# Two key tiles' scores, then two tiles' value products: an attention loop of a two-layer transformer on one NeuronCore

## The chip, the core and the metric

The kernel runs on one core of one Trainium2 chip. The metric is the time of one execution on the device in microseconds (us). Lower is better. The engines are named PE (TensorE, matrix products; PEld is its weight load), ACT (ScalarE), DVE (VectorE), POOL (GpSimd) and SP (SyncE, which here issues DMA transfers).

## The reference

The work is two layers, each an attention block and a gated feed-forward block, with the same weights in both layers. The sequence has 2048 rows of width 448. There are 16 query heads of width 28, and one key and one value head that all of them share.

```python
def _A_ref(x, wq, wk, wv, wo):               # x: 1 x 2048 x 448, H = 16, Dh = 28
    q = (x @ wq).reshape(B, S, H, Dh).transpose(0, 2, 1, 3)
    k = x @ wk                                # 2048 x 28, shared by the heads
    v = x @ wv
    scores = einsum("bhqd,bkd->bhqk", q, k) * (Dh ** -0.5)
    p = softmax(scores, axis=-1)
    o = einsum("bhqk,bkd->bhqd", p, v)
    return o.transpose(0, 2, 1, 3).reshape(B, S, H * Dh) @ wo

def _B_ref(x, w_gate, w_up, w_down):          # inner width 1792
    return (silu(x @ w_gate) * (x @ w_up)) @ w_down

x = x + _A_ref(layernorm(x), wq, wk, wv, wo)
x = x + _B_ref(layernorm(x), w_gate, w_up, w_down)
x = x + _A_ref(layernorm(x), wq, wk, wv, wo)
x = x + _B_ref(layernorm(x), w_gate, w_up, w_down)
```

All values are float32. Products that need more than one reduced-precision pass split an operand in a high and a low part and add up three products.

## The kernel before

**Engines and order.** The order on each engine is the order in which the program issues its instructions; nothing is rescheduled. Engines wait for each other through semaphores that follow from the use of tiles and banks. PSUM has eight banks of 128 x 512 float32. In the attention stage two groups of three banks, `threes[0]` and `threes[1]`, and two single banks, `banks[6]` and `banks[7]`, are in use.

**Attention, `scores`.** A group `i` is one block of 512 query rows and four of the 16 heads, so there are 16 groups in `GR` for each layer. A step `n = 16 i + kt` handles key tile `kt` (128 keys) of group `i`. In it:

- `step(n)`, line 564: 12 score products in three passes of four. The four heads lie in four row strips of the array (32 x 128 each) and run beside each other. Three heads write the banks of `threes[n % 2]`, the fourth writes bank 7. Then ACT takes the exponential of bank 7 into `pt1` (line 570), and of the three banks into `pt` (line 571).
- `between_steps(n)`: only at `kt == 10`, and only for groups after which four groups of one block of queries are complete (three times in each layer): the output projection (`outproj`, line 548) of 48 products into the score banks which are free, with four additions to the residual `xres` on DVE (line 552). In two of these blocks PE also transposes parts of a normalised tile (`flip`).
- `pv(n - 2)`, line 601: four products of exponentials and values, one for each head, in four column strips of the array (128 x 32 each), added up in bank 6 over the 16 key tiles of the group. The values carry a column of ones, whose sums are the softmax's denominators.
- After a group's last tile, `post(i)` copies bank 6 to SBUF (line 614, DVE) and sends the denominators through four small DMA transfers to a tile `rs` (line 617). Two steps later `rest` compares and inverts them on DVE (lines 623 to 625), spreads them with two transfers through DRAM (`rd` and `o`, lines 627 and 628), and POOL multiplies and splits the result (lines 635, 133 and 134).

**Beside the steps.** At `kt == 4` SP loads the raw queries of group `i + 2` (`stack`, `qraw`, line 377), at `kt == 7` POOL splits them (`parts`), and at `kt == 9` a transfer adds rows of maxima (`rows`, line 388). In groups 11, 12 and 13, `weights` loads and splits weights of the feed-forward block at `kt == 8`. In groups 5, 13 and 14 parts of a layer norm are issued, one in each step from `kt == 6`: four times statistics on DVE (lines 213 and 214), then `scale` on POOL (`rstd`, lines 218 and 219). In groups 5 and 13 the four `apply` on DVE (line 226) follow, from `kt == 11`; the first of them waits for `rstd`.

The program has a second copy of the whole (`full`), which is skipped at run time unless a check on the denominators asks for it; it does not run in the executions shown here.

The functions that the change touches:

Of the kernel before, what the change touches and what calls it, by code (L numbers as in the profile page):

```python
# [8 lines left out]
F32 = mybir.dt.float32  # L9
F32R = mybir.dt.float32r  # L10
AF = mybir.ActivationFunctionType
ALU = mybir.AluOpType
# [3 lines left out]
P = 128  # L16
# [6 lines left out]
NT = S // P  # L23
NC = S // 512
# [29 lines left out]
def forward(  # L54
# [14 lines left out]
    nc = tc.nc  # L69
    fine, least, whole = fine or (None, None, None)  # L70
    KC = NC
# [14 lines left out]
    phase, banks, threes, live, turn = ExitStack(), [], [], set(), {}  # L86
# [33 lines left out]
    def halves(name):  # L120

        return pers.tile([P, 2, 512], F32R, tag="halves", name=name, bufs=2)
# [9 lines left out]
    def split(hi, lo, raw):  # L132
        nc.gpsimd.tensor_scalar(hi, raw, 1.0, 0.0, ALU.mult, ALU.add)
        nc.gpsimd.tensor_tensor(lo, raw, hi, ALU.subtract)
# [6 lines left out]
    vsb = pers.tile([P, NT, 32], F32, name="vsb")  # L141
# [151 lines left out]
    def between(*pos):  # L293

        for i, po in enumerate(pos):
            nc.scalar.copy(seen[:, i : i + 1], po[:, 0:1])  # L296

    GR = [(c, g) for c in range(NC) for g in range(NG)]

    class Attention:  # L300
# [208 lines left out]
        def finish(self):  # L509

            wide.append(ALL)
            if self.layer:
                nc.scalar.activation(warm, halfn[:, 0:1], AF.Exp)
                if not full:
                    self.fetch((3, 2))
                    self.fetch((0, 1))
            while self.seen < len(self.order):
                self.project()
            if not full:
                self.maxima(NC - 1, (6,))  # L520
            for n in sorted(self.when):
                for f in self.when[n]:
                    f()
            self.advance(len(self.steps), NM + KC * LEAD)
            wide.append(LOW)

        def scores(self, ff):
            next(switch)
            with tc.tile_pool(name=f"at{self.layer}", bufs=1) as wp:
                woh = wp.tile([P, NG, D], F32R, name="woh")  # L530
                wol = wp.tile([P, NG, D], F32R, name="wol")
                on, accs, pts = {}, {}, {}
                todo, due = [], {}

                def load_wo(z):
# [20 lines left out]
                def step(n):  # L556

                    i, kt = divmod(n, NT)
                    three, one = threes[n % 2], banks[7]
                    q, k, ks = qts[i % 3], keys[kt // 4], slice(P * (kt % 4), P * (kt % 4) + P)  # L560
                    for z, (kp, part) in enumerate(((0, 0), (1, 0), (0, 1))):
                        for j in range(4):
                            js = slice(32 * j, 32 * j + 32)
                            nc.tensor.matmul(  # L564
                                three[:, j, :] if j < 3 else one, k[js, kp, ks], q[js, part, :],
                                start=(z == 0), stop=(z == 2), tile_position=(32 * j, 0),
                            )
                    pt = wp.tile([P, 3, 512], F32, name="pt", bufs=3)
                    pt1 = wp.tile([P, 512], F32, name="pt1", bufs=2 if full else 3)
                    nc.scalar.activation(pt1, one, AF.Exp, scale=SCALE)  # L570
                    nc.scalar.activation(pt, three, AF.Exp, scale=SCALE)  # L571
                    pts[n] = [*(pt[:, j, :] for j in range(3)), pt1]

                def between_steps(n):

                    i, kt = divmod(n, NT)
                    free, one = threes[(n + 1) % 2], banks[7]
                    if full:
                        self.lent = free[:, 0, :]
                        self.advance(KC)  # L580
                        if kt == 11 and i + 1 < len(GR):
                            self.places[i + 1](free[:, 1, :])
                    if not todo or kt != 10:
                        return
                    c = todo.pop()
                    ks = list({8: (0, 1), 12: (2, 3)}.get(i, ()))
                    adds = []
                    for t in (1, 2, 3):
                        if ks:
                            flip(got, X0, [ks.pop(0)], one)  # L590
                        adds.append(outproj(c, t, free[:, t - 1, :]))
                    for f in adds:
                        f()
                    outproj(c, 0, one)()

                def pv(n):
                    i, kt = divmod(n, NT)
                    if kt == 0:
                        accs[i] = banks[6]
                    for j in range(4):  # L600
                        nc.tensor.matmul(  # L601
                            accs[i][32 * j : 32 * j + 32, :], vsb[:, kt, :], pts[n][j],
                            start=(kt == 0), stop=(kt == NT - 1), skip_group_check=True,
                        )
                    del pts[n]
                    if kt == NT - 1:
                        due[n + 4] = post(i)

                def post(i):

                    c, g = GR[i]
                    out2 = halves("o2").bitcast(F32)
                    oraw, rb = out2[:, 0, :], out2[:, 1, :]
                    nc.vector.tensor_copy(oraw, accs.pop(i))
                    rs = wp.tile([P, 16], F32, name="rs", bufs=2)
                    for j in range(4):
                        nc.sync.dma_start(rs[32 * j : 32 * j + 32, :], oraw[32 * j + DH : 32 * j + DH + 1, :])

                    def rest():
                        if fine is not None:  # L620
                            under = wp.tile([P, 16], F32, name="under", bufs=2)
                            for bound, op in ((LIMIT, ALU.is_lt), (1.0 / LIMIT, ALU.is_gt)):
                                nc.vector.tensor_scalar(under, rs, bound, None, op)
                                nc.vector.tensor_tensor(fine, fine, under, ALU.mult)
                        nc.vector.reciprocal(rs, rs)
                        rd = dram.tile([4, 512], F32, name="rd", bufs=2)
                        nc.sync.dma_start(rd.rearrange("j (p n) -> (j p) n", n=16), rs)
                        nc.sync.dma_start(rb, rd[:, None, :].to_broadcast([4, 32, 512]))
                        if g == 0:
                            on[c] = (  # L630
                                wp.tile([P, NG, 512], F32R, name="onh"),
                                wp.tile([P, NG, 512], F32R, name="onl"),
                            )
                        oh, ol = on[c]
                        nc.gpsimd.tensor_tensor(rb, oraw, rb, ALU.mult)  # L635
                        split(oh[:, g, :], ol[:, g, :], rb)
                        if g == NG - 1 and c < NC - 1:
                            todo.append(c)

                    return rest  # L640
# [6 lines left out]
                last = NT * len(GR)  # L647
                for n in range(last):
                    i, kt = divmod(n, NT)
                    if kt == 4 and 2 < i + 2 < len(GR):  # L650
                        self.stack(i + 2)
                    if kt == 7 and 2 < i + 2 < len(GR):
                        self.parts(i + 2)
                    if kt == 9 and 2 < i + 2 < len(GR) and not full:
                        self.rows(i + 2)
                    if i in (2, 3) and kt == 8:
                        load_wo(i - 2)
                    if n == NT and ff.nxt:
                        ff.nxt.below(nc.sync)
                    if kt == 8 and 10 < i <= 11 + FG:  # L660
                        ff.W[i - 11] = weights(i - 11)
                    step(n)
                    if not full:
                        between_steps(n)
                    if n > 1:
                        pv(n - 2)
                    if full:
                        between_steps(n)
                    if n in due:
                        due.pop(n)()  # L670
                    if i in (5, 13, 14) and kt > 5:
                        for f in {5: fs, 13: fs1, 14: ff.second[0][:5]}[i][kt - 6 : kt - 5]:
                            f()
                for n in (last - 2, last - 1):
                    pv(n)
                self.lent = None
                next(switch)
                ff.X[0] = X0
# [236 lines left out]
    for c in range(1, NC):  # L915
        fs, got = norm_steps(c)
        n = 4 * c - 4
# [38 lines left out]
```

## Time and profile before

| what | value |
|---|---|
| median of 3 runs | 2043.97 us (2043.89 to 2044.6) |
| the profiled execution | 2044.63 us |
| its span, first to last instruction | 2042.9 us |
| mean granted clock of TensorE | 0.995 |
| layer 0, first to last exponential | 68.6 to 591.0 us of the span |
| layer 1, first to last exponential | 1078.3 to 1601.0 us of the span |

In a row of the timeline stand the start in us from the start of the span, the duration in us, the engine, the line of the kernel, the operation, its output and input by the names of tiles with their shapes, and the number of instructions that the row takes together. In brackets stands how long the engine had been idle, and what released it. In a row of the costliest groups stand the count, then the busy time in us, the mean duration in ns, and idle time in us. In a row of the stretches stand the stretch in us, its length, the busy time of PE, PEld, DVE, ACT and POOL with the number of instructions, the granted clock of TensorE, and the DMA's share and rate.

### The profile page before, as it was taken

The page shows a single profiled execution, that of the slowest core. Times are in us where ns is not written, and L with a number is a line of the kernel's source. Part 1 is how long each engine was busy: PE and PEld are TensorE (multiplying, and loading weights), DVE is VectorE, ACT ScalarE, POOL GpSimd, SP SyncE. Part 2 cuts the span into 40 slices and gives each one's busy share as a digit, 9 for nine tenths or more (in the row PEclk, how much of TensorE's full clock was granted, in tenths as well). Part 3 has the DMA queues.
Part 4 walks back from the last instruction along what each step waited for, and adds up shares of the span by engine and source line. Part 5 has one row for each costly group of instructions (what it writes and reads, how often), then busy time and mean ns, then how long its engine had stood idle before and what let it go on. Part 6 is the DMA issues. An engine that isn't in the chain of part 4 may idle for free.

```text
span 2042.9 us, 43566 instructions
## 1 busy us (share of the span) xinstructions
PE 2013.0 (99%) x18577; PEld 1263.8 (62%) x18577; DVE 460.8 (23%) x892; ACT 1311.6 (64%) x2152; POOL 534.3 (26%) x599
## 2 busy tenths in 40 slices
PE   8999999999999999999999999999999999999997
PEld 6433434334358999999883334343343689988887
DVE  7200101002115232322451001010011242222322
ACT  4799897997964333333348998979979443333332
POOL 4222111021312333333351221101132123233320
PEclk9999999999999999999999999999999999999999
DMA  5101000011100111100030110000110000111102
GB/s 162 50 22 28 21 13 22 14 35 26 32 12 19 31 31 31 31 24 18 21 105 23 29 30 12 22 12 22 33 45 10 27 16 16 31 31 31 31 1 75
DMA packets 76516, 63.47 MB, mean 31 GB/s; under 512 B 22904, under 2 KB 63224, under 8 KB 76312
## 3 DMA queue, kind: packets, MB, share of 16 engines
q1 hardware_dynamic: 76040, 60.56, 10.4%
q8 instruction: 147, 2.41, 0.5%
q14 instruction: 57, 0.47, 0.1%
q10 hardware_dynamic: 272, 0.03, 0.0%
HBM read 47.72 MB, written 12.32 MB: 29 GB/s over the span
## 4 chain that ended last, share of the span: by engine, by line
PE 48%; ACT 46%; issue 1%; DVE 1%; DMA 0%; POOL 0%; ACTq 0%; POOLq 0%; DVEq 0%
PE bank L289 39%; ACT pt L571 31%; ACT pt L570 15%; PE bank L269 3%; PE three L548 2%; PE bank L548 2%; PE bank L243 1%; PE bank L601 1%; PE three L564 1%; DVE xres L735 0%; DVE sg L821 0%; DVE h L825 0%; DVE xn L226 0%; ACT h L822 0%; ACT sg L820 0%
## 5 line engine op out<-in xcount | busy, mean ns | idle before, releaser
L571 ACT ACTIVATE pt<-three 128x1536 f32<-128x1536 f32 x512 | 741.3, 1448 | 0.0
L601 PE MATMUL bank<-pt,vsb 128*32 128x512 f32 x4096 | 547.5, 607 | 0.5 <-ACT pt L571 0.5
L564 PEld LDWEIGHTS three<-qstack,keys 32*128 32x128 f32 x4608 | 253.5, 184 | 448.5 <-ACT pt L570 392.4
L564 PE MATMUL three<-qstack,keys 32*128 32x512 f32 x4608 | 500.4, 427 | 0.5 <-ACT pt L571 0.4
L564 PE MATMUL bank<-qstack,keys 32*128 32x512 f32 x1536 | 494.4, 427 | 4.0 <-ACT pt L570 4.0
L289 PE MATMUL bank<-xh,wgh 64*128 64x512 f32 x1728 | 456.4, 390 | 0.4
L289 PE MATMUL bank<-xh,wgl 64*128 64x512 f32 x1404 | 374.0, 390 | 0.0
L570 ACT ACTIVATE pt<-bank 128x512 f32<-128x512 f32 x512 | 305.9, 597 | 77.9 <-PE bank L564 71.0
L289 PE MATMUL bank<-xl,wgh 64*128 64x512 f32 x1296 | 341.6, 390 | 0.0
L289 PE MATMUL bank<-wdh,h 64*128 64x448 f32 x1792 | 335.3, 364 | 1.4 <-ACT h L822 0.8
L289 PEld LDWEIGHTS bank<-xh,wgh 64*128 64x128 f32 x1728 | 270.1, 184 | 20.1 <-DVE xl L250 1.5
L289 PEld LDWEIGHTS bank<-wdh,h 64*128 64x128 f32 x1792 | 248.0, 184 | 17.9 <-issue 2.7
L739 POOL TENSOR_TENSOR xres<-stage,xres 128x448 f32<-128x448 f32 x108 | 127.4, 1199 | 499.6 <-ACT stage L738 499.6
L635 POOL TENSOR_TENSOR o<-o 128x512 f32<-128x512 f32 x32 | 41.1, 1283 | 826.7 <-DMA o<-rd 756.8
L564 PEld LDWEIGHTS bank<-qstack,keys 32*128 32x128 f32 x1536 | 244.6, 184 | 5.4 <-ACT pt L570 5.1
L296 ACT COPY seen<-bank 128x1 f32<-128x1 f32 x664 | 82.2, 163 | 247.1 <-PE bank L289 244.1
L289 PEld LDWEIGHTS bank<-xh,wgl 64*128 64x128 f32 x1404 | 222.0, 184 | 14.5
L289 PE MATMUL bank<-wdl,h 64*128 64x448 f32 x896 | 222.8, 367 | 0.0
L820 ACT ACTIVATE sg<-bank 128x512 f32<-128x512 f32 x112 | 67.3, 601 | 220.5 <-PE bank L289 215.4
L289 PEld LDWEIGHTS bank<-xl,wgh 64*128 64x128 f32 x1296 | 201.7, 184 | 11.1
L601 PEld LDWEIGHTS bank<-pt,vsb 128*32 128x32 f32 x4096 | 80.9, 108 | 191.0 <-issue 176.3
L821 DVE TENSOR_TENSOR sg<-bank,sg 128x512 f32<-128x512 f32 x112 | 77.5, 692 | 501.1 <-ACT sg L820 492.1
(113 smaller groups left out, 1722.7 us busy)
## 6 DMA issues: line engine op xcount, KB each, us to landing
o<-rd SPq DMA_DIRECT2D x32, 256.0 KB
qd<-stage SPq DMA_DIRECT2D x32, 224.0 KB
qraw<-qd SPq DMA_DIRECT2D x128, 56.0 KB
wdr<-in_B_w_down_dram SPq DMA_DIRECT2D x28, 224.0 KB
wr<-in_B_w_gate_dram SPq DMA_DIRECT2D x28, 192.0 KB
wr<-in_B_w_up_dram SPq DMA_DIRECT2D x28, 192.0 KB
out_dram<-xres SPq DMA_DIRECT2D x16, 224.0 KB
xres<-in_A_x_dram SPq DMA_DIRECT2D x3, 896.0 KB
```

The lines of the kernel that those rows point to most:

```text
L269: nc.tensor.matmul(po, a, b, start=(i == 0), stop=(i == len(seq) - 1))
L289: nc.tensor.matmul(po, a, b, start=start, stop=stop, skip_group_check=True)
L296: nc.scalar.copy(seen[:, i : i + 1], po[:, 0:1])
L548: nc.tensor.matmul(po[:, 0:D], a[:, g, ts_], b[:, g, :], start=(g + z == 0), stop=(g == NG - 1 and z == 2))
L564: nc.tensor.matmul(three[:, j, :] if j < 3 else one, k[js, kp, ks], q[js, part, :], start=(z == 0), stop=(z == 2), tile_position=(32 * j, 0),)
L570: nc.scalar.activation(pt1, one, AF.Exp, scale=SCALE)
L571: nc.scalar.activation(pt, three, AF.Exp, scale=SCALE)
L601: nc.tensor.matmul(accs[i][32 * j : 32 * j + 32, :], vsb[:, kt, :], pts[n][j], start=(kt == 0), stop=(kt == NT - 1), skip_group_check=True,)
L635: nc.gpsimd.tensor_tensor(rb, oraw, rb, ALU.mult)
L739: nc.gpsimd.tensor_tensor(r, s, r, ALU.add)
L820: nc.scalar.activation(sg, pg[0], AF.Silu)
L821: nc.vector.tensor_tensor(sg, pg[1], sg, ALU.mult)
```

## The change

The loop is now over pairs of key tiles, `d = n // 2`. The scores of both tiles of a pair are issued one after the other, and then the value products of both tiles of the pair before (`pv(d - 1)`), eight products which add up in one bank. Banks 6 and 7 now take turns as the single score bank: tile `2d` writes its fourth head to `single(d)`, tile `2d + 1` to `single(d + 1)`. The value products of the pair before go to `single(d)`, once the exponential of tile `2d` has read it. DVE copies (first pair of a group) or adds this bank to a sum in SBUF, `accs[i]`, which takes the place of the copy in `post`. `between` and `rest` come once for a pair, after the value products; `rest` is issued three pairs after the pair that ends its group. `pt` has four buffers instead of three and `pt1` four instead of three. The last `maxima` uses bank 7 instead of bank 6.

In the order of the engines, the same numbers of PE, ACT and POOL instructions remain, and DVE has 256 additions or copies of 128 x 512 where it had 32 copies. On SP, the loads of `qraw` of a group now stand ahead of the two transfers of `rest`, not behind them.

```diff
-                self.maxima(NC - 1, (6,))
+                self.maxima(NC - 1, (7,))
...
+                single = lambda d: banks[6 + d % 2]
...
-                    three, one = threes[n % 2], banks[7]
+                    three, one = threes[n % 2], single(n // 2 + n)
...
-                    pt = wp.tile([P, 3, 512], F32, name="pt", bufs=3)
-                    pt1 = wp.tile([P, 512], F32, name="pt1", bufs=2 if full else 3)
+                    pt = wp.tile([P, 3, 512], F32, name="pt", bufs=4)
+                    pt1 = wp.tile([P, 512], F32, name="pt1", bufs=4)
...
-                def between_steps(n):
-                    i, kt = divmod(n, NT)
-                    free, one = threes[(n + 1) % 2], banks[7]
+                def between(d):
+                    i, kt = divmod(2 * d, NT)
+                    free, one = threes[0], single(d + 1)
...
-                def pv(n):
-                    i, kt = divmod(n, NT)
+                def pv(d):
+                    i, kt = divmod(2 * d, NT)
+                    po = single(d + 1)
+                    for n in (2 * d, 2 * d + 1):
+                        for j in range(4):
+                            nc.tensor.matmul(
+                                po[32 * j : 32 * j + 32, :], vsb[:, n % NT, :], pts[n][j],
+                                start=(n == 2 * d), stop=(n > 2 * d), skip_group_check=True,
+                            )
+                        del pts[n]
                     if kt == 0:
-                        accs[i] = banks[6]
-                    for j in range(4):
-                        nc.tensor.matmul(
-                            accs[i][32 * j : 32 * j + 32, :], vsb[:, kt, :], pts[n][j],
-                            start=(kt == 0), stop=(kt == NT - 1), skip_group_check=True,
-                        )
-                    del pts[n]
-                    if kt == NT - 1:
-                        due[n + 4] = post(i)
+                        accs[i] = halves("o2").bitcast(F32)
+                        nc.vector.tensor_copy(accs[i][:, 0, :], po)
+                    else:
+                        nc.vector.tensor_tensor(accs[i][:, 0, :], po, accs[i][:, 0, :], ALU.add)
+                    if kt == NT - 2:
+                        due[d + 3] = post(i)
...
-                    out2 = halves("o2").bitcast(F32)
+                    out2 = accs.pop(i)
                     oraw, rb = out2[:, 0, :], out2[:, 1, :]
-                    nc.vector.tensor_copy(oraw, accs.pop(i))
...
                     step(n)
-                    if not full:
-                        between_steps(n)
-                    if n > 1:
-                        pv(n - 2)
-                    if full:
-                        between_steps(n)
-                    if n in due:
-                        due.pop(n)()
+                    d, odd = divmod(n, 2)
+                    if odd:
+                        if d:
+                            pv(d - 1)
+                        between(d)
+                        if d in due:
+                            due.pop(d)()
...
-                for n in (last - 2, last - 1):
-                    pv(n)
+                pv(last // 2 - 1)
```

More of the change, by code (lines that the diff above doesn't have):

```diff
@@ L572, in step @@
                     pts[n] = [*(pt[:, j, :] for j in range(3)), pt1]
-                def between_steps(n):
-                    i, kt = divmod(n, NT)
-                    free, one = threes[(n + 1) % 2], banks[7]
+                def between(d):
+                    i, kt = divmod(2 * d, NT)
+                    free, one = threes[0], single(d + 1)
                     if full:
                         self.lent = free[:, 0, :]
-                        self.advance(KC)
-                        if kt == 11 and i + 1 < len(GR):
+                        self.advance(2 * KC)
+                        if kt == 10 and i + 1 < len(GR):
                             self.places[i + 1](free[:, 1, :])
```

## The prediction

> **What bounds the kernel now.** The page came first, for shares and mean durations.
>
> ```profile
> span 2042.9 us, 43566 instructions
> PE 2013.0 (99%) x18577; PEld 1263.8 (62%) x18577; DVE 460.8 (23%) x892; ACT 1311.6 (64%) x2152; POOL 534.3 (26%) x599
> ...
> L571 ACT ACTIVATE pt<-three 128x1536 f32<-128x1536 f32 x512 | 741.3, 1448 | 0.0
> L601 PE MATMUL bank<-pt,vsb 128*32 128x512 f32 x4096 | 547.5, 607 | 0.5 <-ACT pt L571 0.5
> ...
> L570 ACT ACTIVATE pt<-bank 128x512 f32<-128x512 f32 x512 | 305.9, 597 | 77.9 <-PE bank L564 71.0
> ```
>
> There are 512 steps (2 layers, 16 groups, 16 key tiles), and the change touches nothing outside them. Both PE and ScalarE look full there, so the timeline of steady steps has to say which one sets the pace. It reads: start, duration, engine, line.
>
> ```profile
> 402.37 0.16 PEld L601 LDWEIGHTS bank<-pt,vsb 128*32 128x32 f32 x8 [0.37 <-issue]
> 402.56 0.63 ACT L570 ACTIVATE pt<-bank 128x512 f32<-128x512 f32 x1
> 402.83 0.61 PE L601 MATMUL bank<-pt,vsb 128*32 128x512 f32 x4
> 403.37 0.19 PEld L564 LDWEIGHTS three<-qstack,keys 32*128 32x128 f32 x3 [0.84 <-ACT pt L570]
> 403.71 0.40 PE L564 MATMUL three<-qstack,keys 32*128 32x512 f32 x3
> 403.95 0.39 PE L564 MATMUL bank<-qstack,keys 32*128 32x512 f32 x1
> 404.27 0.16 PEld L601 LDWEIGHTS bank<-pt,vsb 128*32 128x32 f32 x8 [0.36 <-issue]
> 404.46 0.60 ACT L570 ACTIVATE pt<-bank 128x512 f32<-128x512 f32 x1
> ...
> 404.95 1.45 ACT L571 ACTIVATE pt<-three 128x1536 f32<-128x1536 f32 x1
> ...
> 405.27 0.19 PEld L564 LDWEIGHTS three<-qstack,keys 32*128 32x128 f32 x3 [0.84 <-ACT pt L570]
> ...
> 406.35 0.60 ACT L570 ACTIVATE pt<-bank 128x512 f32<-128x512 f32 x1
> ```
>
> PE goes round without a gap: scores 403.37 to value products 404.27 is 0.90, products to scores 1.00 (402.37 to 403.37, 404.27 to 405.27). The row at 403.37 names L570 as releaser, but its end comes 0.18 us earlier there (403.19) and 0.21 earlier at 405.27, while PE's 1.00 stays: PE's own stream is the bound, at 1.90 a step. ScalarE follows close behind, and its floor shows where it was behind once:
>
> ```profile
> 399.43 1.45 ACT L571 ACTIVATE pt<-three 128x1536 f32<-128x1536 f32 x1
> 399.67 0.69 DVE L614 COPY o<-bank 128x512 f32<-128x512 f32 x1 [24.64 <-PE bank L601]
> 400.47 0.16 PEld L601 LDWEIGHTS bank<-pt,vsb 128*32 128x32 f32 x8 [0.36 <-DVE o L614]
> 400.75 0.60 ACT L570 ACTIVATE pt<-bank 128x512 f32<-128x512 f32 x1
> 401.23 1.48 ACT L571 ACTIVATE pt<-three 128x1536 f32<-128x1536 f32 x1
> ...
> 430.15 0.69 DVE L614 COPY o<-bank 128x512 f32<-128x512 f32 x1 [25.08 <-PE bank L601]
> 460.57 0.69 DVE L614 COPY o<-bank 128x512 f32<-128x512 f32 x1 [24.40 <-PE bank L601]
> ```
>
> L571 to the next L570 takes 1.32 here (1.33 from 401.23 to 402.56), L570 to L571 0.48 (0.49 at 404.46), so ScalarE could do a step in 1.82 and PE holds it at 1.90. One group takes 30.42 us between the last two rows: 3.80 for each pair of steps.
>
> **The change on PE alone: fewer turns.** A products pass of four takes 0.46 (402.37 to 402.83); the second lasts 0.54 until scores start, so turning back costs about 0.1. The first scores pass takes 0.34 (403.37 to 403.71), the second 0.24. For a pair PE now needs: 0.34, four passes of 0.24, 0.32 until products start, then 3 x 0.45 and 0.54, together 3.51 instead of 3.80. ScalarE's floor for a pair is 2 x 1.82 = 3.64. If nothing else held, the pair would go at 3.64. [...]
>
> **The wait that replaces it.** Scores of tile 2d+1 go to the same three-bank tile as those of 2d-1, which L571 of 2d-1 must have read; that read ends just after L570 of 2d starts. Before, one tile's products stood between any two score blocks and covered this. Now scores of 2d+1 stand directly behind those of 2d, so PE waits, and both tiles' products queue behind the wait, with scores of 2d+2 behind those. The latencies come from the start of the loop, where the same waiting shows:
>
> ```profile
> 68.00:70.00 2.00, 0.73 (x9) 0.48 (x9) 1.90 (x4) 1.38 (x2) 1.62 (x2) 0.94 0.00 0
> 70.00:72.00 2.00, 1.89 (x16) 1.01 (x12) 0.13 (x1) 2.00 (x3) 0.00 (x0) 0.50 0.12 37
> ```
> ```profile
> 68.62 0.60 ACT L570 ACTIVATE pt<-bank 128x512 f32<-128x512 f32 x1 [2.87 <-DVE two L403]
> 69.27 0.18 PEld L564 LDWEIGHTS bank<-qstack,keys 32*128 32x128 f32 x1 [2.44 <-ACT pt L570]
> 69.61 0.47 PE L564 MATMUL bank<-qstack,keys 32*128 32x512 f32 x1
> ```
>
> PE starts 0.05 after ScalarE's end, and a first pass after a wait takes 0.34 even with no turn. So the loop, from one end of L571 (odd tile) round to that of two pairs later: 0.05 wait, 0.90 scores of the odd tile, 3 x 0.45 + 0.54 = 1.89 products, 1.09 scores of the even tile until its L570 (403.37 to 404.46), then 0.49, 1.33 and 0.49 until the next odd L571 starts, 1.45 until it ends: 7.69, or 3.85 for a pair. That is 0.05 more than 3.80. Of 256 pairs some 240 are plain (6 hold output projections, 4 start the layers, 6 stand at stalls told below): 240 x 0.05 = +12. Bounds: if the odd tile's first pass needs only the 0.24 of a running stream, 3.80, so 0; with product passes of 0.50 (half of 1.00) and 0.20 from ScalarE to PE, 4.00, so +48. I stay near the first chain, since each link has a row of its own.
>
> Two new waits aren't late. Products wait for L570 of 2d (0.60 + 0.05), which ends before PE gets there. The bank is freed by VectorE's add: products' last pass ends 1.35 + 0.61 after their start, then an estimated 0.1, 0.69 (L614 handles the same tile; the add also reads SBUF) and 0.11 (400.36 to 400.47): 2.86, whereas scores of 2d+3 come 2.95 to 3.1 after that start. Slack is 0.1 to 0.3, so whatever blocks VectorE now reaches PE. The 256 adds and copies, 177 us of VectorE work, otherwise lie beside PE.
>
> **VectorE blocked behind a norm.** In group 13 VectorE has four L226 to issue from key tile 11 on. The first waits for GpSimd's L219, and two of them now stand ahead of the add for tiles 10 and 11.
>
> ```profile
> 502.72 0.69 DVE L614 COPY o<-bank 128x512 f32<-128x512 f32 x1 [13.75 <-PE bank L601]
> 507.09 0.18 DVE L623 TENSOR_SCALAR under<-rs 128x16 f32<-128x16 f32 x1 [3.68 <-DMA rs<-o]
> 507.81 0.24 DVE L625 RECIPROCAL rs<-rs 128x16 f32<-128x16 f32 x1
> 527.33 1.78 DVE L226 TENSOR_SCALAR xn<-xres,mv,rstd 128x448 f32<-128x448 f32 x4 [16.39 <-POOL rstd L219]
> ```
> ```profile
> 514.86 1.28 POOL L635 TENSOR_TENSOR o<-o 128x512 f32<-128x512 f32 x1 [30.05 <-DMA o<-rd]
> 526.28 1.01 POOL L219 TENSOR_TENSOR rstd<-rstd,halfn 128x4 f32<-128x4 f32 x1
> ```
>
> That wait of 16.39 was free. The reciprocals move two adds later: 2 x 3.85 + 0.96 (507.09 to 508.05) after the group's last add, instead of 4.64. From there GpSimd's chain is as long as before: 6.8 to L635 and 12.4 to the end of L219, so 27.9 after the last add. Two L226 (0.9) and the add (0.69) make 29.5, but the add is due six pairs after, at 23.1: 6.4 late, 6.1 beyond the slack. Twice (two layers): +12. Group 5 has the same order without weights:
>
> ```profile
> 241.23 0.24 DVE L625 RECIPROCAL rs<-rs 128x16 f32<-128x16 f32 x1
> ```
> ```profile
> 255.87 1.02 POOL L219 TENSOR_TENSOR rstd<-rstd,halfn 128x4 f32<-128x4 f32 x1
> ```
>
> There 15.4 lie between the two ends: 8.7 + 15.4 + 1.6 = 25.7 against 23.1, late by up to 2.3 beyond the slack. But SP's queue now issues the four loads of qraw ahead of rd and of the load of o, so these may land sooner by the 1.9 that this stretch exceeds group 13's: 0 to 2.3, I take 1, twice: +2. The small four-row rs transfers themselves are no wait any more, two adds stand before their use.
>
> **Clock.** In the rows at 68 the granted clock falls to 0.50 after PE sat idle 2.44 us. A stall of 6.1 should do that too; the work after it then runs at half speed for some 4 us, losing 2 (0 to 3.4): twice, +4. [...]
>
> **Output projections.** Six blocks stand between products and the next scores.
>
> ```profile
> 221.29 0.37 PE L548 MATMUL bank<-woh,onl 128*128 128x448 f32 x1
> 221.77 0.62 DVE L552 TENSOR_TENSOR xres<-bank,xres 128x448 f32<-128x448 f32 x1 [0.75 <-PE bank L548]
> ```
>
> Products used to run while VectorE added the last tile; now scores wait for it: 0.11 + 0.62 + 0.05, say 0.8, of which 0.3 comes back as the next two score blocks run without a wait: 6 x 0.5 = +3. Everything else (four buffers for pt, bank 7 for the last maxima, the copy of L614 gone) I cost at nothing, -3 to +3 for the layers' starts.
>
> **Sum** against the profiled execution's 2044.6 (0.6 above the median of 2044.0, which is within the runs shown): 12 + 12 + 2 + 4 + 3 = 33, so 2077.6; less the 0.6, 2077.
>
> **Rivals.** *Faster:* the odd tile's wait is short enough that ScalarE binds at 3.64: 240 x 0.16 = -38, with the stalls' +12 and +3 left, 2021; with the stalls hidden too, 2006. It decides once the loop above is under 7.28, so 0.41 of its links would have to be wrong. For it stands PE's 3.51; against it, that each link has its row. [...] *Same:* the loop comes out at its lower bound, 3.80, and GpSimd's chain is early enough that only the blocks' 3 remain: about 2047. *Much slower:* PE's clock falls not twice but again and again, because every pair now has a wait. In the trace a low stretch lasted from 70 to beyond 76, costing about 3.4; once in each of 32 groups is 32 x 3.4 = 109, with the 29 others 2182; eight such drops give 2100. Against it: waits in plain pairs sum to 3.85 - 3.51 = 0.34, under a tenth of PE's time. *The change doesn't do what it says:* PE's order in the changed program shows 24 score products, then 8 value products into the bank just freed, so no.
>
> **Numbers.** Forecast 0.70 (own range 2052 to 2100, from the bounds: links 0 to +30, since both far ends at once are unlikely, stalls +10 to +17, clock 0 to +7, blocks 0 to +3), faster 0.14, same 0.06, much slower 0.10. With 0.2% (4 us) as what can be told from no change: faster 0.14, same 0.07, slower 0.79. Eight in ten: own range less its edges (0.66), the case of no change (0.06) and the near part of the much slower one (0.06), with a few hundredths of the faster one's near end: 2038 to 2106.
>
> **What would show it.** Right: L570 spaced about 3.85 for a pair, alternating short and long; an idle PEld ahead of odd scores, released by L571; ScalarE idle ahead of even L570, waiting for PE; in group 13 an idle PE of some 6 us released by the add, and a low clock behind it. Wrong: pairs at 3.65 with ScalarE never idle (faster), VectorE's add as the common releaser of scores, or a granted clock under 1.00 throughout.

## The result, and the profile after

The changed kernel takes 2070.63 us (median of 4 runs, 2069.83 to 2071.57) where the kernel before takes 2044.28 (4 runs). The ratio is 1.0124, with a 95% interval of 1.0112 to 1.0137. That is slower by 26 us; the forecast was 2077, slower by 33. The profiled execution took 2071.57 us, its span is 2069.8 and its mean granted clock 0.993 of full speed.

The page of the changed kernel, shares and then the groups of the steps (count, busy time, mean ns, idle time ahead and its releaser). The exponentials are now lines 571 and 572, scores 565, products 604, the add 613.

```profile
PE 1997.6 (97%) x18577; PEld 1296.5 (63%) x18577; DVE 612.2 (30%) x1116; ACT 1298.6 (63%) x2152; POOL 533.5 (26%) x599
...
L565 PE MATMUL three<-qstack,keys 32*128 32x512 f32 x4608 | 497.7, 426 | 33.5 <-ACT pt L572 31.6
L565 PE MATMUL bank<-qstack,keys 32*128 32x512 f32 x1536 | 492.2, 427 | 15.9 <-DVE o L613 13.5
L604 PE MATMUL bank<-pt,vsb 128*32 128x512 f32 x4096 | 497.0, 603 | 0.5 <-ACT pt L571 0.3
...
L571 ACT ACTIVATE pt<-bank 128x512 f32<-128x512 f32 x512 | 308.5, 602 | 116.4 <-PE bank L565 112.0
...
L613 DVE TENSOR_TENSOR o<-bank,o 128x512 f32<-128x512 f32 x224 | 154.8, 691 | 645.3 <-PE bank L604 632.4
```

The score rows of the kernel before were:

```profile
L564 PE MATMUL three<-qstack,keys 32*128 32x512 f32 x4608 | 500.4, 427 | 0.5 <-ACT pt L571 0.4
L564 PE MATMUL bank<-qstack,keys 32*128 32x512 f32 x1536 | 494.4, 427 | 4.0 <-ACT pt L570 4.0
```

Products are busy 50 us less (497.0 after 547.5), which points to fewer turns; the ends of products are modelled, so it is a rough measure. PE as a whole is busy 15 us less (1997.6 after 2013.0). But PE now idles ahead of scores: 31.6 us for ScalarE's read of the three banks, and 13.5 for VectorE's add, where it idled 0.5 and 4.0 before.

The timeline in steady steps (start, duration, engine, line; in brackets idle time and releaser), and then the copies that begin two groups:

```profile
401.77 1.47 ACT L572 ACTIVATE pt<-three 128x1536 f32<-128x1536 f32 x1
402.12 0.19 PEld L565 LDWEIGHTS three<-qstack,keys 32*128 32x128 f32 x3 [0.84 <-ACT pt L571]
402.31 0.69 DVE L613 TENSOR_TENSOR o<-bank,o 128x512 f32<-128x512 f32 x1 [3.04 <-PE bank L604]
403.21 0.60 ACT L571 ACTIVATE pt<-bank 128x512 f32<-128x512 f32 x1
403.30 0.50 PE L565 MATMUL three<-qstack,keys 32*128 32x512 f32 x3 [0.21 <-ACT pt L572]
404.21 0.16 PEld L604 LDWEIGHTS bank<-pt,vsb 128*32 128x32 f32 x8 [0.37 <-ACT pt L571]
404.21 1.92 PE L604 MATMUL bank<-pt,vsb 128*32 128x512 f32 x16
405.51 1.48 ACT L572 ACTIVATE pt<-three 128x1536 f32<-128x1536 f32 x1
406.06 0.19 PEld L565 LDWEIGHTS three<-qstack,keys 32*128 32x128 f32 x3 [0.84 <-ACT pt L571]
407.04 0.19 PEld L565 LDWEIGHTS three<-qstack,keys 32*128 32x128 f32 x3 [0.44 <-ACT pt L572]
407.14 0.60 ACT L571 ACTIVATE pt<-bank 128x512 f32<-128x512 f32 x1 [0.16 <-PE bank L565]
407.64 1.44 ACT L572 ACTIVATE pt<-three 128x1536 f32<-128x1536 f32 x1
408.97 0.60 ACT L571 ACTIVATE pt<-bank 128x512 f32<-128x512 f32 x1
409.44 1.47 ACT L572 ACTIVATE pt<-three 128x1536 f32<-128x1536 f32 x1
410.88 0.60 ACT L571 ACTIVATE pt<-bank 128x512 f32<-128x512 f32 x1
...
436.95 0.69 DVE L611 COPY o<-bank 128x512 f32<-128x512 f32 x1 [3.27 <-PE bank L604]
467.61 0.69 DVE L611 COPY o<-bank 128x512 f32<-128x512 f32 x1 [3.27 <-PE bank L604]
```

The loop of the prediction can be walked. L572 of an odd tile ends at 403.24 (401.77 + 1.47). The next odd scores start at 403.30, with PE idle and L572 named as the releaser; products follow at 404.21, even scores at 406.06. ScalarE waits for these, starts L571 at 407.14, then L572, L571, and the next odd L572 at 409.44, which ends at 410.91. That is 7.67 for two pairs. The even L571 rows at 403.21, 407.14 and 410.88 are 3.93 and 3.74 apart: long and short in turn. The pair in between closes a second loop in the same way: its odd scores start at 407.04, 0.05 after L572 ends (405.51 + 1.48). There the row shows only the weight load as idle. A group takes 30.66 us between the last two rows, so 3.83 for a pair where it was 3.80.

The place where VectorE is blocked, group 13, in the timeline of layer 0 and then in the stretches of layer 1 (in these, the decimal after POOL's count is the granted clock):

```profile
525.35 0.69 DVE L613 TENSOR_TENSOR o<-bank,o 128x512 f32<-128x512 f32 x1 [2.50 <-PE bank L604]
533.16 1.01 POOL L219 TENSOR_TENSOR rstd<-rstd,halfn 128x4 f32<-128x4 f32 x1
534.21 0.94 DVE L226 TENSOR_SCALAR xn<-xres,mv,rstd 128x448 f32<-128x448 f32 x2 [8.17 <-POOL rstd L219]
535.06 0.68 DVE L613 TENSOR_TENSOR o<-bank,o 128x512 f32<-128x512 f32 x1
535.80 0.79 PE L565 MATMUL bank<-qstack,keys 32*128 32x512 f32 x1 [5.25 <-DVE o L613]
537.37 3.61 PE L604 MATMUL bank<-pt,vsb 128*32 128x512 f32 x16
...
1284.48 0.50 PE L565 MATMUL bank<-qstack,keys 32*128 32x512 f32 x1 [0.75 <-DVE o L613]
...
1560.82 0.79 PE L565 MATMUL bank<-qstack,keys 32*128 32x512 f32 x1 [7.54 <-DVE o L613]
```
```profile
1554.00:1558.00 4.00, 0.00 (x0) 0.00 (x0) 0.00 (x0) 0.61 (x1) 3.83 (x4) 0.57 0.03 4
1558.00:1562.00 4.00, 1.18 (x9) 0.83 (x9) 2.38 (x5) 0.00 (x0) 2.43 (x6) 0.50 0.00 0
1562.00:1566.00 4.00, 4.00 (x31) 1.10 (x29) 0.37 (x1) 1.94 (x2) 0.00 (x0) 0.65 0.00 0
```

VectorE stands before L226 until GpSimd ends L219; the add behind it, due some 3.7 us after the one at 525.35, comes at 535.06; PE idles 5.25 us there and 7.54 in layer 1 (the row at 1560.82; the one at 1284.48 is group 5 of layer 1, 0.75). Then the clock is at half: eight products take 3.61 instead of the 1.92 of a steady pair.

Group by group (from the even L571 of its first tile to that of the next group's), the 26.9 us between the two profiled executions are: group 13, +8.3 and +10.1; group 5, +0.25 and +1.5; groups with an output projection, +2.5 for six; all others about +0.25 each; the first groups of the layers, -0.3 and -1.2; the rest of the program, about +1, which is within the 1.7 us by which executions of the changed kernel differ.

### The profile page after: what moved, and what is told of

Same layout as the page of the kernel before. It is cut to its first block, busy times and chain, and to the rows that moved or that the text cites. A ratio compares the mean times of both kernels' runs of the same rounds, so it can differ in the third digit from the quotient of the medians.

```text
span 2069.8 us, 43968 instructions
## 1 busy us (share of the span) xinstructions
PE 1997.6 (97%) x18577; PEld 1296.5 (63%) x18577; DVE 612.2 (30%) x1116; ACT 1298.6 (63%) x2152; POOL 533.5 (26%) x599
## 3 DMA queue, kind: packets, MB, share of 16 engines
q1 hardware_dynamic: 76040, 60.56, 10.1%
## 4 chain that ended last, share of the span: by engine, by line
PE 70%; ACT 17%; issue 7%; DVE 2%; DMA 2%; POOL 2%; SPq 0%; ACTq 0%; POOLq 0%; DVEq 0%
PE bank L289 38%; PE bank L604 12%; PE three L565 11%; ACT pt L572 10%; ACT pt L571 7%; PE bank L269 3%; PE three L549 2%; PE bank L549 2%; PE bank L243 1%; PE bank L565 1%; DMA o<-rd 1%; DVE xn L226 0%; DVE xl L250 0%; POOL rstd L219 0%; DMA kt<-stage 0%
## 5 line engine op out<-in xcount | busy, mean ns | idle before, releaser
L572 ACT ACTIVATE pt<-three 128x1536 f32<-128x1536 f32 x512 | 748.2, 1461 | 0.0
L565 PE MATMUL three<-qstack,keys 32*128 32x512 f32 x4608 | 497.7, 426 | 33.5 <-ACT pt L572 31.6
L565 PE MATMUL bank<-qstack,keys 32*128 32x512 f32 x1536 | 492.2, 427 | 15.9 <-DVE o L613 13.5
L604 PE MATMUL bank<-pt,vsb 128*32 128x512 f32 x4096 | 497.0, 603 | 0.5 <-ACT pt L571 0.3
L571 ACT ACTIVATE pt<-bank 128x512 f32<-128x512 f32 x512 | 308.5, 602 | 116.4 <-PE bank L565 112.0
L613 DVE TENSOR_TENSOR o<-bank,o 128x512 f32<-128x512 f32 x224 | 154.8, 691 | 645.3 <-PE bank L604 632.4
L604 PEld LDWEIGHTS bank<-pt,vsb 128*32 128x32 f32 x4096 | 107.4, 109 | 252.7 <-issue 163.0
L642 POOL TENSOR_TENSOR o<-o 128x512 f32<-128x512 f32 x32 | 41.1, 1284 | 850.5 <-DMA o<-rd 498.4
```

Of the source, the lines that this page charges most:

```text
L565: nc.tensor.matmul(three[:, j, :] if j < 3 else one, k[js, kp, ks], q[js, part, :], start=(z == 0), stop=(z == 2), tile_position=(32 * j, 0),)
L604: nc.tensor.matmul(po[32 * j : 32 * j + 32, :], vsb[:, n % NT, :], pts[n][j], start=(n == 2 * d), stop=(n > 2 * d), skip_group_check=True,)
L613: nc.vector.tensor_tensor(accs[i][:, 0, :], po, accs[i][:, 0, :], ALU.add)
```

## The experiments

**The theory:** two mechanisms. In plain pairs the odd tile's scores wait until ScalarE has read their three banks, and so close a loop of 3.83. In group 13 (and a little in 5) the add that frees the score bank is queued behind L226, which waits for GpSimd. **Rivals:** VectorE's 224 new adds are the bound everywhere; or ScalarE's own pace is, and the odd wait is only its shadow; or the kernel before was held by ScalarE too, so that the order of PE's work mattered little.

**The four L226 five key tiles later.** They move from the last tiles of groups 5 and 13 to the first four tiles of groups 6 and 14.

```diff
-                        for f in {5: fs, 13: fs1, 14: ff.second[0][:5]}[i][kt - 6 : kt - 5]:
+                        for f in {5: fs[:5], 13: fs1[:5], 14: ff.second[0][:5]}[i][kt - 6 : kt - 5]:
...
+                    if i in (6, 14) and kt < 4:
+                        {6: fs, 14: fs1}[i][5 + kt]()
```

> The changed kernel with the four normalising steps of groups 5 and 13 (line 226) issued in the first four steps of groups 6 and 14, when GpSimd's rstd is long there. Theory (VectorE's adds queue behind a waiting normalising step): groups 13 lose their 8.3 and 10.1 us, group 5 of layer 1 its 1.3 us, the granted clock stays whole there, so 2070.6 - 19.5 = 2051. Rival (the pair's own loop does it, and the stalls of group 13 are only where waiting time collects): the same time comes back in other groups, within 4 us of 2070.6.

Measured: 2052.44 us, ratio 1.0040 (1.0026 to 1.0054). Group 13 takes 30.63 and 30.67, a plain group's time. The timeline of VectorE, and a row of the waits (us in total, times, longest):

```profile
532.97 0.69 DVE L613 TENSOR_TENSOR o<-bank,o 128x512 f32<-128x512 f32 x1 [3.22 <-PE bank L604]
534.62 0.51 DVE L226 TENSOR_SCALAR xn<-xres,mv,rstd 128x448 f32<-128x448 f32 x1 [0.96 <-POOL rstd L219]
```
```profile
PE three L565 <- ACT pt L572: 30.9, 126, 2.2
```

The add comes before L226 now, and the wait of PE for L613 (13.5 us) is gone from the waits. The wait of scores for L572 is left as it was (30.9, was 31.6). So 18 of the 26 us were two stalls, one in each layer, behind a queued instruction, and not the order of products and scores.

**The denominators one pair earlier.** The same stall from its other end: GpSimd's chain starts earlier.

```diff
-                        due[d + 3] = post(i)
+                        due[d + 2] = post(i)
```

> The changed kernel with the reciprocals and all that follows them issued two pairs after the pair that ends a group, not three. Theory (GpSimd's chain starts at the reciprocals, and they came one pair too late): rstd comes 3.8 us sooner, the stall of group 13 shrinks by 3.8 us in each layer and the one of group 5 goes, perhaps the clock no longer falls: 2070.6 - 9 to - 14, 2057 to 2062. VectorE now waits for the small transfers right before an add, 3.7 us after the last add against 3.83 to the next, so at most 0.3 us in each of 32 groups, +0 to +10. Rival (the stall comes from the weights' transfers and not from the reciprocals): group 13 keeps its length of 38.8 to 40.6 us, about 2071 to 2080.

Measured: 2060.54 us, ratio 1.0074 (1.0058 to 1.0091). Group 5 is down to a plain group's 30.65, group 13 to 34.89 and 34.95. In the timeline of PE and in the stretches:

```profile
533.14 0.50 PE L565 MATMUL bank<-qstack,keys 32*128 32x512 f32 x1 [2.00 <-DVE o L613]
534.03 3.10 PE L604 MATMUL bank<-pt,vsb 128*32 128x512 f32 x16
```
```profile
534.00:538.00 4.00, 4.00 (x25) 1.34 (x28) 0.69 (x1) 1.94 (x2) 0.23 (x2) 0.58 0.00 0
```

One pair earlier takes 3.3 us off the idle time in layer 0 (5.25 to 2.00) and 5.4 in layer 1 (7.54 to 2.17), on average 4.3, somewhat more than the 3.8 of a pair that the chain through GpSimd gives. The 2.00 that stay are still followed by half the clock: 0.58 in the stretch after, and products at 3.10.

**The add over half of the columns.** The other half is left out; VectorE's work is shorter and nothing else.

```diff
-                        nc.vector.tensor_tensor(accs[i][:, 0, :], po, accs[i][:, 0, :], ALU.add)
+                        nc.vector.tensor_tensor(accs[i][:, 0, 0:256], po[:, 0:256], accs[i][:, 0, 0:256], ALU.add)
```

> The changed kernel with an addition on VectorE over half of the columns alone (the other half of the sums is left out), so the bank comes free about 0.3 us sooner. Theory (odd scores wait for ScalarE's read of the three banks, VectorE's add is next behind it): a plain pair stays at 3.83 us, and only the places where VectorE was late gain: 2066 to 2071. Rival (the add holds the bank and is what odd scores really wait for): a pair goes to about 3.66, 240 x 0.17 = 41 less, 2030.

Measured: 2070.81 us, ratio 1.0128 (1.0111 to 1.0144), and a plain group at 30.66: no change. VectorE's adds set nothing in plain pairs. The first rival falls.

**Half of the exponential of three banks.** (From here on, each kernel ran once. Executions of one kernel above differ by 2 to 5 us.) If the odd wait sets the pace, a shorter L572 must shorten the pair, and the kernel before, which PE holds, must not gain. Products read the computed half twice.

```diff
-                    nc.scalar.activation(pt, three, AF.Exp, scale=SCALE)
-                    pts[n] = [*(pt[:, j, :] for j in range(3)), pt1]
+                    nc.scalar.activation(pt[:, :, 0:256], three[:, :, 0:256], AF.Exp, scale=SCALE)
+                    pts[n] = [*(pt[:, j, None, 0:256].to_broadcast([P, 2, 256]) for j in range(3)), pt1]
```

In the changed kernel:

> The changed kernel with the exponential of the three banks over half of the columns (256 of 512 in each bank; the value products read that half twice), so a step of ScalarE takes about 1.2 instead of 1.82 us, and PE's and VectorE's work is unchanged. Theory: the loop over ScalarE's read falls to 7.67 - 2 x 0.64 = 6.4 us for two pairs, and the next one behind it binds, the one over VectorE's add: products' start to the add's end 2.78, 0.05, scores 0.90, together 3.73 us a pair. Time 2070.6 - 250 x 0.10 - some of the stalls = 2043. Rival (PE's own stream with its turns still binds): 3.83 a pair, 2070.

In the kernel before:

> The kernel before with the same halved exponential of the three banks. Theory (PE's stream of 1.90 us a step is the bound before, ScalarE's 1.82 is not): a pair of steps stays at 3.79 to 3.80 us and the time at 2040 to 2044. Rival (ScalarE's exponentials were the bound): a step goes down towards PE's and the time falls by some tens of us.

Measured: 2035.32 us in the changed kernel, 3.69 for a pair, 8 us and 0.04 less than expected; 2042.24 in the kernel before, with groups at the old 30.4 (L614 at 429.05 and 459.47). ScalarE was not the bound before, and is in the loop after; the third rival falls. The timeline of the changed kernel with the half shows what binds next:

```profile
402.94 0.16 PEld L604 LDWEIGHTS bank<-pt,vsb 128*32 128x32 f32 x8 [0.36 <-ACT pt L571]
404.99 0.69 DVE L613 TENSOR_TENSOR o<-bank,o 128x512 f32<-128x512 f32 x1 [2.99 <-PE bank L604]
405.73 0.18 PEld L565 LDWEIGHTS bank<-qstack,keys 32*128 32x128 f32 x1 [0.17 <-DVE o L613]
406.63 0.16 PEld L604 LDWEIGHTS bank<-pt,vsb 128*32 128x32 f32 x8 [0.37 <-ACT pt L571]
```

Products at 402.94, the add at 404.99, scores into the freed bank at 405.73, products at 406.63: 3.69. This is the loop over VectorE, 0.14 under the other one.

**The same, and half of the add.** Both halves together.

> As the one before, and the add on VectorE over half of the columns as well. Theory: now neither ScalarE nor VectorE holds PE, and what is left is PE's own stream: 0.34, four passes of 0.23, 0.32, and products of 1.85, together 3.45 us a pair: 2070.6 - 250 x 0.38 = 1976, less what the stalls lose. Rival (turning costs no less in twos than it did for each tile): 3.80 a pair, 2060.

Measured: 2010.27 us, 3.60 for a pair (groups of 28.8) and not 3.45: a miss. The timeline:

```profile
403.81 0.19 PEld L565 LDWEIGHTS three<-qstack,keys 32*128 32x128 f32 x3 [0.84 <-ACT pt L572]
404.89 0.60 ACT L571 ACTIVATE pt<-bank 128x512 f32<-128x512 f32 x1 [1.09 <-PE bank L565]
405.54 0.16 PEld L604 LDWEIGHTS bank<-pt,vsb 128*32 128x32 f32 x8 [0.50 <-ACT pt L571]
407.39 0.19 PEld L565 LDWEIGHTS three<-qstack,keys 32*128 32x128 f32 x3 [0.84 <-issue]
```

Even scores 1.08, L571 0.60, 0.05 until products may write the bank that it read, products 1.85: 3.58. A third loop, which the prediction had named as a wait that isn't late, comes up once two others are gone. PE's own 3.51 was not reached by any run, so it stays an estimate; but 3.60 is under the 3.80 of the kernel before, so fewer turns do shorten PE's stream.

**A copy more for each add.** VectorE's loop is lengthened on purpose.

```diff
+                        nc.vector.tensor_copy(accs[i][:, 1, :], po)
                         nc.vector.tensor_tensor(accs[i][:, 0, :], po, accs[i][:, 0, :], ALU.add)
```

> The changed kernel with one more VectorE copy of the product bank ahead of each of the 224 adds, 0.69 us each; VectorE then is busy some 38% of the time. Theory (the bank's release has a slack of 0.1 us in the pair): the loop over VectorE becomes 3.73 + 0.6 to 0.7 = 4.33 to 4.43 us a pair, 224 pairs of 256: + 0.55 x 224 = 123, 2180 to 2205. Rival (VectorE has two thirds of its time free, so it is hidden): 2071 to 2075.

Measured: 2161.76 us; slower, but below what was expected. The timeline of VectorE (the copy is line 613 here, the add 614):

```profile
405.62 0.69 DVE L613 COPY o<-bank 128x512 f32<-128x512 f32 x1 [3.01 <-PE bank L604]
406.23 0.68 DVE L614 TENSOR_TENSOR o<-bank,o 128x512 f32<-128x512 f32 x1
...
414.20 0.69 DVE L613 COPY o<-bank 128x512 f32<-128x512 f32 x1 [3.00 <-PE bank L604]
418.48 0.69 DVE L613 COPY o<-bank 128x512 f32<-128x512 f32 x1 [3.00 <-PE bank L604]
```

The pair is now 4.28, which is about VectorE's loop of 3.69 and the 0.61 by which the add starts after the copy. The first pair of each group has no second instruction and stays near 3.7, so a group takes 33.7. The expectation took 0.55 more for each of the 224 pairs (a loop of 3.73 and a copy of 0.6 to 0.7), where 0.45 came (4.28 less 3.83); besides, the groups with an output projection grew by 2.2 to 2.4 us and group 13 by 2.3 and 2.9, less than the 3.1 of a plain group.

**A third set of score banks.** This takes away what makes odd scores wait. The eight banks that the program lays out are all in use here (two sets of three, and banks 6 and 7), so a control comes first: one head's scores are left out, so that a set is two banks; ScalarE makes a plain copy in place of the head's exponential, and products use another head's. The control has two sets, the test three; a last one also halves the add.

```diff
-                        for j in range(4):
+                        for j in (0, 1, 3):
...
+                    nc.scalar.copy(filler, source)
...
-                    three, one = threes[n % 2], single(n // 2 + n)
+                    three, one = threes[n % 3], single(n // 2 + n)
```

The last change shown is only in the runs with three sets. Control, three sets, three sets with half the add:

> A control for the next run: the changed kernel with one of the four heads' scores left out (its value products read another head's exponentials), so a step needs two banks and one instead of three and one; the ScalarE time that is saved is filled by a copy of 512 columns ahead of the exponential of the two banks. Tiles take turns on two sets of two banks. Theory: the wait of odd scores for the set two tiles back is as in the changed kernel, a pair takes 3.80 to 3.87 us. Rival: the wait is not the cause, and a pair takes the ScalarE floor of about 3.66 or PE's 3.45.

> As the control, but tiles take turns on three sets of two banks, so odd scores need what ScalarE read one tile earlier. Theory: the wait for ScalarE's read goes, and the next loop binds, over VectorE's add: 3.73 us a pair, 0.1 less than the control, some 25 us. Rival (the wait is not what costs): the same as the control within 5 us.

> As the one before with the add over half of the columns. Theory: nothing is left but ScalarE's own work, about 3.66 us a pair (or as long as its three instructions of a step take back to back), another 15 to 20 us less. Rival: 3.73 as without it, and VectorE was not the next bound.

Measured: 2107.5, 2088.9 and 2090.43 us. These kernels can only be compared with each other: PE idles some 12 us at each layer's start, so their first groups take 41 to 44 us instead of about 32. The third set brings 18.6, some 11 of it in plain groups and those with a projection; half the add then brings nothing. A pair takes 3.88, 3.83 and 3.83, where 3.80 to 3.87, 3.73 and 3.66 (or ScalarE's own three instructions) were expected: the first is a narrow miss, the second a clear one, and the third came out by its bracket. In the timeline of ScalarE with three sets (line 574 is the exponential of one bank, 575 the copy, 576 the exponential of the set) its three instructions stand back to back:

```profile
399.83 0.85 ACT L574 ACTIVATE pt<-bank 128x512 f32<-128x512 f32 x1
400.31 0.89 ACT L575 COPY filler<-source 128x512 f32<-128x512 f32 x1
400.82 1.30 ACT L576 ACTIVATE pt<-three 128x1024 f32<-128x1024 f32 x1
401.75 0.86 ACT L574 ACTIVATE pt<-bank 128x512 f32<-128x512 f32 x1
```

So a step is 1.92 here and a pair 3.83 by ScalarE alone: the copy of 512 columns made it longer than the 1.82 of the real kernel, and these three runs can't tell the odd wait from ScalarE's pace well. Two more have a copy of 400 columns, so that ScalarE alone could go faster.

```diff
-                    nc.scalar.copy(filler, source)
+                    nc.scalar.copy(filler[:, 0:400], source[:, 0:400])
```

> Control, as the two-set control before it (one head's scores are left out, and ScalarE makes a plain copy in its place), with the copy cut from 512 to 400 columns, so that ScalarE's three instructions need an estimated 1.80 us a step (0.11 less) and no longer set the pace by themselves. Theory (the odd tile's scores wait until ScalarE has read their set): the copy stands twice in a loop over two pairs, so a pair goes down by 0.11, from 3.94 to about 3.83, and the time from 2107 to about 2080. Rival (the odd scores' wait is only a shadow of ScalarE's own pace): also shorter by twice the cut of one step, 0.22 a pair, to 3.72, about 2053.

> The control with the copy of 400 columns, and three sets of two banks instead of two. Theory: the wait for ScalarE's read goes, ScalarE alone could do 3.60 a pair, and the next loop, over VectorE's add that frees the single bank, sets the pace at about 3.70 a pair: some 25 to 32 us less than the control with the same copy, about 2050 to 2058, with odd scores released by VectorE's add. Rival (the wait is a shadow of ScalarE's pace): no difference from the control with the same copy.

Measured: 2083.4 and 2061.15 us, 3.79 and 3.69 for a pair. The shorter copy alone took the control's pair from 3.88 (not the 3.94 that the expectation starts from) to 3.79: 0.09, near the 0.11 of a loop that holds the copy twice in two pairs (an estimate: 112 of 512 columns of the 0.51 us from the copy's start to the next instruction's, 400.31 to 400.82 above), and not the 0.22 of ScalarE's own pace. The waits, control first (its line 576 reads the set), then three sets (line 618 is the add):

```profile
PEld three L568 <- ACT pt L576: 148.6, 244, 12.5
```
```profile
PEld bank L568 <- DVE o L618: 55.6, 212, 7.2
```

With two sets scores wait for ScalarE's read 244 times. With three sets that wait is not in the list, and scores wait for VectorE's add, in the loop of 3.69 found above. Of the 25 us expected at least, 22 came, nearly all in plain groups (30.33 to about 29.54). The wait is real and not a shadow of ScalarE's pace: it goes with a bank, while ScalarE's work is the same. The second rival falls.

No run found a version of the full computation faster than the kernel before. The best one is the first, at 2052.

## Why the prediction was right, and where its terms were off

The direction and both mechanisms held, and the number is 6 us high. By its own steps, in the order of its sum of +33 against the 26.9 between the profiled executions:

- **Plain pairs, +12 forecast, about +7.5 measured** (0.25 for each of some 30 groups). The loop is the predicted one, link by link, at 7.67 instead of 7.69. The terms that were off are the products, which take 1.85 (404.21 to 406.06) and not 3 x 0.45 + 0.54 = 1.89, and the even scores (1.08 for 1.09), against a few hundredths more in other links. So a pair gained 0.03 and not 0.05: a small difference of two numbers near 3.8, which hundredths of a microsecond decide.
- **VectorE behind the norm, group 13, +12 forecast, 12.8 measured** as PE's idle time (5.25 + 7.54). The chain of waits was right, and the run with L226 later shows that it is the cause. That the sum comes so close is in part luck: twice 6.1 was forecast, and the two differ by 2.3; in the run with half the add they are 5.26 and 4.87.
- **Clock, +4 forecast, about +5 measured.** Group 13 lost 8.3 + 10.1 = 18.4; less 12.8 idle and 0.5 of plain pairs, 5.1 are left for work at half clock. Half the clock (0.50 in 1558 to 1562) came with the waits of 5.25 and 7.54, and not with the short ones of plain pairs (0.21; the clock is at 1.00 from 80 to 530); the forecast, too, counted the two stalls alone. The 2.00 in the run with the earlier denominators was enough too (0.58 after it). The forecast's 4 us of half clock after a stall were the author's estimate, and no row of the kernel before shows them; after the change the low clock ends about 5.0 us after the stall in layer 0 (0.50 from 534 to 540, 0.79 in 540 to 542) and 4.0 in layer 1 (0.65 in 1562 to 1566). (The 2.44 of the prediction is the idle time of the weight load; PE's products sat idle for 2.13 there.)
- **Group 5, +2 forecast, +1.2 measured** beyond plain pairs. The layers differ: in one the add is not late at all, in the other PE idles 0.75.
- **Output projections, +3 forecast, about +1 measured** beyond plain pairs. Of the net 0.5 each, 0.2 is there. The dear link is the wait of scores for VectorE's addition (L553): 2.2 us in all six, 0.37 each, where 0.8 was taken. The forecast also left out a gain: before, PE idled 0.76 ahead of the transposes in four of the six blocks, released by L570, and that is gone; these four cost no more than plain groups, and the two others (group 4) 0.5 and 0.8 beyond them.
- **The starts, 0 forecast, about -2 measured** beyond plain pairs; inside the bounds of -3 to +3 that were named. Part of it may be luck with the clock: at the layers' starts its low stretches (0.50) lasted 6.83 us in the kernel before and 3.41 in the changed one, and the first groups took 32.6 and 32.9 us before and 32.3 and 31.7 after. That the clock did it is an estimate: 3.41 us at half the clock are 1.7 us of work.
- **The waits called not late.** VectorE's add is not, in plain pairs: half the add changed nothing. Its loop is 0.14 under the one that binds, on average inside the slack of 0.1 to 0.3 that was given, and from products' start to the add's start it takes 2.05 (402.94 to 404.99 in the run with half the exponential) where 2.06 was taken with an estimated 0.1 in it; but the slack goes in turn: odd scores start some 0.3 after the add's end in the long pairs (403.00 to 403.30) and only 0.05 to 0.1 after it in the short ones. Products' wait for the even L571 is not late either, but only by 0.25: it binds at 3.58 once the two loops above it are shortened.

The rivals: *faster* asked for the loop under 7.28, and it is 7.67. Fewer turns show in the 3.60 of the run with both halves, under the 3.80 of the kernel before; but the loop that binds goes through ScalarE, and the time did not follow. *Same* would have needed GpSimd's chain early: with L226 out of the way the kernel is still at 1.0040. *Much slower* did not come, since no plain pair's wait lowered the clock (1.00 from 80 to 530 and from 1096 to 1550).

## What to carry to other kernels

An order that spares an engine work also changes which reads have to end before its next writes: walk each buffer's loop (writer, reader, the next writer) in the new order, and compare these loops with the engine's own stream before counting the saving. Here three loops and ScalarE's own pace lie within 0.25 us of each other (3.83, 3.69, 3.58 and an estimated 3.64), and so removing one wait is worth only the step to the next. And an instruction put into the loop of a tight buffer makes everything queued ahead of it on its engine critical: one norm in each layer, which waited for free before, cost 18 of the 26 us.

## What the runs showed of the hardware

In the middle of a layer, an idle time of PE of 2.00 us was followed by a granted clock of 0.58 (group 13 with the earlier denominators, 534 to 538), while after 0.75 the clock stayed at 1.00 (group 5 of layer 1 in the changed kernel, 1284 to 1288). In the changed kernel's profiled execution the clock was at 0.50 for 3.41 us at each layer's start, for 6.83 in group 13 of layer 0 and for 10.24 in that of layer 1; in the kernel before, for 6.83 at each layer's start. In the kernels with three heads, where PE idles some 12 us at the layers' starts, the mean granted clock was 0.984 to 0.988, against 0.993 in the changed kernel.

In layer 1 of the changed kernel the clock fell while PE was idle: it is at 0.57 in 1554 to 1558, where PE runs nothing. With the earlier denominators it fell after the idle time: it is at 1.00 in 530 to 534, the stall ends at 533.14, and 534 to 538 has 0.58. In these runs a stall cost its own length and something more: group 13, less its stall and a plain group's time, lost 2.8 us with the stall of 5.25, 2.3 with that of 7.54, and 2.2 and 2.1 with those of 2.00 and 2.17. Here the longer idle time did not cost more clock.
